# Scaled sums for C2 and decayed B, one bf16 product for the numerators, four-tile K features and loads as list steps in a fused state-space and linear-attention kernel

## The chip, the cores and the metric

One core of a Trainium2 chip. The time is the device time of one execution in microseconds, the median of the runs shown. The kernel is one program without a loop at run time; its engines (TensorE or PE, VectorE or DVE, ScalarE or ACT, GpSimd or POOL, SyncE or SP) each work through their own instructions in order and wait for one another by semaphores.

## What is computed

x has 2048 rows of 512. Two branches work on it, and a gate per row mixes them:

```python
g = sigmoid((x * gate_w).sum(-1))                      # one number per row
# branch A: a diagonal state-space model with complex poles
Lam_bar = exp(dt * Lam);  B_bar = (Lam_bar - 1) / Lam * B
h[t] = Lam_bar * h[t-1] + B_bar @ x[t]
a[t] = 2 * Re(C @ h[t]) + x[t] * Dskip
# branch B: linear attention, 32 heads of 16
pq, pk = q @ w_phi, k @ w_phi                          # per head
phi = concat(softmax(p), softmax(-p))                  # 32 features per head
kv = sum_s phi_k[s] v[s]^T;  z = sum_s phi_k[s]
b = (phi_q @ kv) / (phi_q @ z + 1e-6) @ wo
out = g * a + (1 - g) * b
```

Inputs and output are bf16.

## The kernel before

Rows are split by their index modulo four, so that a tile of 128 rows ("ti", 16 of them) holds rows of one residue, and the recurrence runs as a scan over 512 steps of four rows each. x is loaded transposed (`xT`, DMA transposes on SyncE, L225).

The program is written as small generators, one for each piece of work (`st_k`, `st_g`, `feat_sum`, ...). Each `yield` ends a step. The string `ORDER` (L24) is the list of steps: the loop at L783 takes a token, sets the PSUM banks behind "@" and the engine of a copy or scaling (":D" gives it to VectorE, otherwise ScalarE), and runs the generator to its next yield. So the list fixes the order of every engine's instructions. `F:n` puts n dummy matmuls of 128 columns on TensorE. The pieces that matter here:

- `W`, `f`, `w` fold the 16x16 head matrices into the K and Q weights; `B` (L319) builds the block matrix for that, four products of 128x128.
- `k`, `v`, `q` (L431 to 450) are projections of one tile: four matmuls of 512 columns, then a copy out of PSUM (L117 on ScalarE, L119 on VectorE).
- Features. `x` (L469) is a maximum tree over 16 values in four steps and a subtraction; `n` (L477) the same with minima; `e` (L483) exponentials on ScalarE, one for each tile; `s` (L489) a tree of sums, logarithm and exponential on ScalarE, and the product that normalizes (L500, or L511 for queries, behind which four DMA transposes per group go out on SyncE, L515). K features run for two tiles at a time, eight groups; the first four query tiles also in two groups of two (A, B); the other twelve in three groups of four (X1 to S3). The trees are the lines L464 of the profile.
- `a` (L521) adds a tile's features times values into `kvacc`, and the gate's sums.
- `U`, `P`, `P2`, `P3`, `P4`, `M` compute the poles from the transposed parameters (`vec_n`, `V`); `i` (L400) the rotation tables by sines on ScalarE, with an absolute value on VectorE (L410); `D` (L376) nine sets of diagonal matrices, three products of 1536 elements.
- Decayed B, `LBT`: `p` (L535) multiplies Bn_r and Bn_i by diagonals on TensorE, four matmuls of 256 columns in each of eight steps, and ScalarE copies out (eight copies).
- `g` (L545) applies BrT/BiT and LBT to x into `uv`; `z` (L585) rotates and scans on VectorE; `h` (L617) gets the in-between states.
- C2, the output matrix: `c` (L565), for each of eight parts two matmuls of 512 columns with diagonals and one copy.
- `r`, `b`, `K` derive the matrices for other residues; `y` (L696) forms branch A of a tile in PSUM.
- `o` (L717) is branch B of a tile: numerators and denominators by eight small matmuls in two halves, two logarithms (`ld`), one exponential (`rd`), and on VectorE two products straight from PSUM with the gate's factor RG (L737, 256 elements each), then a DMA transpose on SyncE (L743). `t` (L746) adds the result times Wo to branch A's PSUM, scales by the gate (L754 on ScalarE or L756 on VectorE), and stores.

Loads: before the list runs, ScalarE's queue issues the K weights (`C2r`), `Wc` and `Wv`; SyncE's issues eight x tiles, B twice (plain, and transposed in eight), the other eight x tiles, the Q weights, C and Wo. `vec_n` comes on GpSimd's queue (L256).

Of the kernel before, what the change touches and what calls it, by code (L numbers as in the profile page):

```python
# [10 lines left out]
ALU = mybir.AluOpType  # L11
# [25 lines left out]
a5 z2 g300 xA s6 s7 q2 z2 s6 s7 z2 g301 g300 xA s7 g311 g301 v12 g310@6 xA g311 z1 nA c11@4 z1 nA eA z2 nB s7 z2 c03@7
c12@2 g310 xB g311 eA q15@5 c12 s6 c03 s7 g310 h01@0 nB q15 g310 sA c10@2 z2 s7 h01 c11 c13@7 xB nB v13@5 z3 xB h11@6
z2 c10 z3 a6 z2 sA z2 h11 q9@0 c02@4 v13 sA q9 xB a6 nB c13 h10@2 q6@5 c02 v15@0 z3 q12@7 q10@6 q8@4 xB v15 sA nB
h21@0 q12 z3 h00@7 q6 q10 q5@5 eB q8 s7 q4@6 a7 sA eB q4 z3 z3 h10 z3 c00@4 q7@2 c00 a7 sB sA r1 sB z3 sB z3 h20@6 sA  # L40
K0@4 sB q7 sA sB z3 q13@2 q5 h31@5 h21 q14@0 sB G h20 h30@6 sA sB h00 q13 h31 sA sB sB sB G h30 Y q11@2 END N1 K2@7 X1
Y o0@5 N1 o1@6 r0 K0 o1 Y X1 N1 X1 q11 Y o0 X1 N1 o0@3 X1 N1 o0 o1@4 y1@1 o1 q14 o1 o0 b1 o0 N2 y0@2 o2@0 o0 K2 X2 o0
E1 o1 E1 E1 y1 E1 o2 X2 K3@7 N2 X2 o2@5 o1 y0 o1 y2@3 S1 o2 o2 o2 K1@6 K1 y2 S1 o2 S1 N2 X2 o2 S1 y3@4 o3@0 y0 r1 X2
N2 K3 S1 S1 N2 y3 r0 S1 S1 S1 o3 o3@5 o3 G y1 y3 y7@6 o3 E2 t0 y2 o3 E2 E2 E2 G t1 o3 t0 y5@7 t2 N3 y4@0 t2 y7 b1 X3
r3 o4@5 N3 S1 S2 S2 o4 o4@2 y5 b0 o4 o4 t1 o3 y4 o4 o5@3 o5 o4 b0 S1 o5@5 S2 t3 o5 b3 S1 o5 r2 o5 y4 y6@1 t3 r2 o4 y7
o6@2 t1 b2 S2 r3 o6 o6@3 y6 b2 o7@4 o6 S2 t0 o5 y5 y6 o5 t4 o6 b3 o7 S2 S2 t2 y8@5 o6 X3 o6 S2 y11@2 t4 X3 t4:A o7@0
o7 N3 y10@3 X3 o7 o6 N3 y11 t5 y10 X3 N3 o7 t6 o7 S2 E3 y8 S2 o8@4 E3 E3 o8 o8@0 o8 S2 o8 o7 t5:D t6:D o8 o8 y10 y8
y9@7 o10@1 o9@4 E3 o9 S3 o9@0 S2 o9 o10 o8 o9 o9 y9 S3 t7 S3 o9 t6 o10@4 y11 o9 o10 S3 o10 y9 o10 S3 o10 y14@0 t8 t7
y13@1 S3 S3 t5:A o11@4 y12@6 y13 o11 t8 o10 S3 o11@5 o11 t9 S3 t9:D S3 y14 t3:A o11 t10 o12@7 o11 S3 o11 t10:D o12
o12@4 o12 o12 y14 o12 o13@5 S3 o13 o13@3 y12 o12 o13 t7 t8:A o13 o11 o13 o12 o14@7 o14 o14@4 o13 o14 t9:A y13 o14 y12  # L50
o14 o14 o15@5 o15 o15@3 y15@7 o15 o15 t11 o15 t11 o13 o14 o15 y15 t12 y15 t10 t12 t14 t14 o15 t11 t12 t13 t14:A t15
t15 t13:D t15:A t13
"""
C2_VECTOR = ()
# [14 lines left out]
def kernel(  # L69
# [92 lines left out]
    nc.scalar.dma_start(out=wk_nat[:], in_=B_wqkv[:, D:2 * D].rearrange("(k p) n -> p k n", p=P))  # L162
    nc.scalar.dma_start(out=Wc[:], in_=B_w_phi.rearrange("(k hl) e f -> (hl e) k f", hl=8))
    nc.scalar.dma_start(out=Wv[:], in_=B_wqkv[:, 2 * D:3 * D].rearrange("(k p) n -> p k n", p=P))
# [13 lines left out]
    RG = const.tile([P, NTI], F32, name="RG")  # L178
    ge = const.tile([P, NTI], F32, name="ge")
# [19 lines left out]
    dg = pBC.tile([P, 9, PT, P], BF16, name="dg")  # L199
# [3 lines left out]
    dgv = pBC.tile([P, 9, PT, 4], BF16, name="dgv")  # L203
# [22 lines left out]

    for ti in range(8):
        x_load(ti)
    nc.sync.dma_start(out=Bn_r[:], in_=A_B_re.rearrange("(j p) d -> p j d", p=P))
    nc.sync.dma_start(out=Bn_i[:], in_=A_B_im.rearrange("(j p) d -> p j d", p=P))  # L230
    for kt in range(KT):
        nc.sync.dma_start_transpose(out=BrT[:, kt, :], in_=A_B_re[:, kt * P:(kt + 1) * P])
        nc.sync.dma_start_transpose(out=BiT[:, kt, :], in_=A_B_im[:, kt * P:(kt + 1) * P])
    for ti in range(8, NTI):
        x_load(ti)
    for j in range(KT):
        nc.sync.dma_start_transpose(out=WTq[:, j, :], in_=B_wqkv[:, j * P:(j + 1) * P])
    for kt in range(KT):
        nc.sync.dma_start_transpose(out=CrT[:, kt, :], in_=A_C_re[:, kt * P:(kt + 1) * P])
        nc.sync.dma_start_transpose(out=CiT[:, kt, :], in_=A_C_im[:, kt * P:(kt + 1) * P])  # L240
    nc.sync.dma_start(out=Wo[:], in_=B_wo.rearrange("(k p) n -> p k n", p=P))

# [7 lines left out]
    make_identity(nc, ident[:])  # L250
    nc.gpsimd.iota(iot[:], pattern=[[1, NC]], base=0, channel_multiplier=0, allow_small_or_imprecise_dtypes=True)
    identf = stg.tile([P, P], F32, name="identf", bufs=1)
    make_identity(nc, identf[:])
# [8 lines left out]
    mask16 = stg.tile([P, 8], F32, name="mask16", bufs=1)  # L262
    nc.vector.tensor_reduce(out=mask16[:], in_=identf[:].rearrange("p (g e) -> p g e", e=16), axis=AX.X, op=ALU.add)
# [13 lines left out]
    def st_W(j):  # L277
        pt = bank([P, KT, P], BF16, "ptw")
        for dtile in range(KT):
            nc.tensor.transpose(pt[:, dtile, :], wk_nat[:, dtile, j * P:(j + 1) * P], ident[:])  # L280
        yield
        evac(WTk[:, j, :], pt[:].rearrange("p a b -> p (a b)"))
        yield
# [35 lines left out]
    def st_B():  # L319
        for kt in range(HG):  # L320
            VT(out=BD[:, kt, :].rearrange("p (g f) -> p g f", f=Dh), in0=Wc[:, kt, :].unsqueeze(1).to_broadcast([P, 8, Dh]),
               in1=mask16[:].unsqueeze(2).to_broadcast([P, 8, Dh]), op=ALU.mult)
            yield
# [52 lines left out]
    def st_D():  # L376
        for k0 in (0, 3, 6):
            if k0 == 0:
                nc.vector.tensor_copy(out=dgv[:].rearrange("p k j f -> p (k j) f"),
                                      in_=dgs[:].rearrange("p k j -> p (k j)").unsqueeze(2).to_broadcast([P, 9 * PT, 4]))  # L380
            VT(out=dg[:, k0:k0 + 3].rearrange("p k j (c f) -> p (k j) c f", f=4),
               in0=ident[:].rearrange("p (c f) -> p c f", f=4).unsqueeze(1).to_broadcast([P, 3 * PT, 32, 4]),
               in1=dgv[:, k0:k0 + 3].rearrange("p k j f -> p (k j) f").unsqueeze(2).to_broadcast([P, 3 * PT, 32, 4]), op=ALU.mult)
            yield
# [15 lines left out]
    def st_i(j):  # L400
# [9 lines left out]
        VS(out=kk_[:].bitcast(mybir.dt.uint32), in0=psi[:].bitcast(mybir.dt.uint32), scalar1=0x7FFFFFFF, scalar2=None, op0=ALU.bitwise_and)  # L410
# [4 lines left out]
    pools = {}  # L415

# [41 lines left out]
    def tree(pool, src5, L, op, nm, key, last_dtype=BF16, groups=NB):  # L458
        cur = src5
        n = Dh  # L460
        while n > 1:
            n //= 2
            t = pool.tile([P, L, groups, n, 4], last_dtype if n == 1 else BF16, name=f"{nm}{n}", bufs=(2 if n == 1 else 1))
            VT(out=t[:], in0=cur[:, :, :, 0:n, :], in1=cur[:, :, :, n:2 * n, :], op=op)  # L464
            cur = t
            live[key] = t
            yield

    def feat_max(p, first, L, nm, small, big):  # L469
        X5 = v5(Xq[:, first:first + L, :])  # L470
        yield from tree(small(), X5, L, ALU.max, f"mx{nm}", ("mx", p))
        EE = big().tile([P, L, NB, 2, 64], BF16, name=f"EE{nm}", bufs=3)
        live["EE", p] = EE
        VT(out=half(EE, 0), in0=X5, in1=live["mx", p][:].to_broadcast([P, L, 8, Dh, 4]), op=ALU.subtract)
        yield
# [351 lines left out]
```

## Time and profile before

| what | value |
|---|---|
| runs shown | 167.51, 167.69, 168.19 us; median 167.69 |
| span of the profiled execution (first to last instruction) | 166.1 us |
| median of the runs less this span | 1.6 us |
| VectorE instructions, busy | 354, 143.7 us |
| ScalarE instructions, busy | 236, 114.8 us |
| TensorE matmuls, busy | 1088, 157.6 us |
| granted TensorE clock, mean | 0.994 |

In the views of the profile a row of a timeline is start, length, engine, line, operation, tiles, shape and count, with idle time and its releaser in brackets. SPq and ACTq are the DMA-issuing instructions of SyncE and ScalarE. A group's row gives the busy time and the mean of one instruction in ns. Times of the profile are those of one execution.

### The profile page before, as it was taken

To read this page: it belongs to the slowest core of one execution; us is meant where nothing else is said; L and a number is where in the kernel's file an instruction comes from. 1 tells how busy PE (TensorE), PEld (TensorE's weight loads), DVE (VectorE), ACT (ScalarE), POOL (GpSimd) and SP (SyncE) were. 2 spreads that over 40 slices of the span, in tenths; PEclk is the share of its full clock that TensorE was granted. 3 is DMA by queue.
4 is the path that set the end of the run, shared out by engine and by line. 5 is a ranking of instruction groups with operands and counts; after the bars stand their busy time and mean duration, and the time that the engine had idled before them with its cause. 6 is when DMAs were issued, how large, how long until landed. Compare 5 with 4: busy or idle time off the path is not lost.

```text
span 166.1 us, 3051 instructions
## 1 busy us (share of the span) xinstructions
PE 157.6 (95%) x1088; PEld 82.3 (50%) x1109; DVE 143.7 (87%) x354; ACT 114.8 (69%) x236; POOL 9.6 (6%) x28
## 2 busy tenths in 40 slices
PE   7689999999999999999999999999999999999990
PEld 7444455455465454454454554545446445445440
DVE  4379999999999999999999999999999996818410
ACT  3389999999898268578965966876888356423331
POOL 8218200000000000000000000000000000000000
PEclk9999999999999999999999999999999999999997
DMA  4969945464444200000000019212296585478542
GB/s 111 267 121 281 142 99 97 95 98 95 95 105 85 98 0 6 0 0 0 0 4 0 0 24 181 52 32 63 65 132 154 162 189 129 119 174 216 128 125 95
DMA packets 50830, 15.94 MB, mean 96 GB/s; under 512 B 46208, under 2 KB 50816, under 8 KB 50816
## 3 DMA queue, kind: packets, MB, share of 16 engines
q1 hardware_dynamic: 48064, 13.77, 39.8%
q10 hardware_dynamic: 2592, 1.98, 4.4%
q8 instruction: 8, 0.13, 0.3%
q14 instruction: 6, 0.05, 0.1%
q0 software_dynamic: 160, 0.01, 0.1%
HBM read 2.64 MB, written 2.10 MB: 29 GB/s over the span
## 4 chain that ended last, share of the span: by engine, by line
PE 84%; DVE 8%; DMA 3%; POOL 2%; issue 1%; ACT 1%; POOLq 0%
PE pgq L552 8%; PE py L750 8%; PE pgq L555 8%; PE py L705 8%; PE pq L429 8%; PE py L706 8%; PE pv L429 5%; PE py L712 4%; PE pk L429 4%; DMA vec_n<-in_A_log_dt_dram 3%; PE kvacc L527 3%; PE pn L728 3%; PE pk L674 2%; PE pk L675 2%; DVE psi L406 2%; DVE mxk L464 1%
## 5 line engine op out<-in xcount | busy, mean ns | idle before, releaser
L429 PEld LDWEIGHTS <-xT 128*128 128x128 bf16 x192 | 18.1, 97 | 20.8 <-DMA xT<-in_A_x_dram 0.7
L136 ACT ACTIVATE EEk<-EEk 128x1024 bf16<-128x1024 bf16 x20 | 21.0, 1070 | 0.8 <-DVE EEk L480 0.8
L737 DVE SCALAR_TENSOR_TENSOR on<-pn,RG,rd 128x256 bf16<-128x256 f32 x32 | 14.4, 474 | 3.2 <-ACT rd L136 1.7
L429 PE MATMUL pv<-Wv,xT 128*128 128x512 bf16 x62 | 16.0, 379 | 0.3 <-DMA xT<-in_A_x_dram 0.2
L750 PE MATMUL py<-Wo,oT 128*128 128x512 bf16 x62 | 15.8, 379 | 0.1
L555 PE MATMUL pgq<-xT,LBT 128*128 128x512 bf16 x60 | 15.5, 379 | 0.2
L429 PE MATMUL pq<-Wq,xT 128*128 128x512 bf16 x61 | 15.6, 379 | 0.1
L429 PE MATMUL pk<-Wk,xT 128*128 128x512 bf16 x61 | 15.1, 379 | 0.2
L136 ACT ACTIVATE EEq<-EEq 128x1024 bf16<-128x1024 bf16 x12 | 11.8, 1044 | 3.3 <-DVE EEq L480 3.3
L136 ACT ACTIVATE ld<-pn 128x16 f32<-128x16 f32 x32 | 4.7, 182 | 12.6 <-PE pn L728 12.6
L706 PE MATMUL py<-Wv,H 128*128 128x512 bf16 x31 | 11.7, 379 | 0.1
L705 PE MATMUL py<-Wk,H 128*128 128x512 bf16 x31 | 11.7, 379 | 0.1
L705 PE MATMUL py<-C2r,H 128*128 128x512 bf16 x31 | 11.7, 379 | 0.0
L117 ACT CAST Xq<-pq 128x512 bf16<-128x512 f32 x16 | 9.2, 589 | 3.6 <-PE pq L429 3.4
L117 ACT CAST uv<-pgq 128x512 bf16<-128x512 f32 x16 | 9.3, 588 | 3.4 <-PE pgq L560 2.3
L706 PE MATMUL py<-C2i,H 128*128 128x512 bf16 x30 | 11.4, 379 | 0.1
L756 DVE TENSOR_SCALAR ot<-py,G 128x512 bf16<-128x512 f32 x5 | 3.7, 747 | 8.4 <-PE py L750 8.4
L117 ACT CAST vx<-pv 128x512 bf16<-128x512 f32 x15 | 8.7, 598 | 2.6 <-PE pv L429 2.6
L754 ACT ACTIVATE ot<-py,G 128x512 bf16<-128x512 f32 x11 | 7.4, 678 | 4.5 <-PE py L750 4.5
L117 ACT CAST Xq<-pk 128x512 bf16<-128x512 f32 x16 | 9.2, 601 | 1.4 <-PE pk L429 1.4
L464 DVE TENSOR_TENSOR smk<-smk 128x512 bf16<-128x512 bf16 (+2 forms) x30 | 9.8, 327 | 0.0
L500 DVE TENSOR_TENSOR EEk<-EEk,rck 128x2048 bf16<-128x2048 bf16 x8 | 9.7, 1214 | 0.0
(179 smaller groups left out, 348.6 us busy)
## 6 DMA issues: line engine op xcount, KB each, us to landing
out_dram<-ot SPq DMA_DIRECT2D x9, 128.0 KB, 2.1
out_dram<-ot ACTq DMA_DIRECT2D x7, 128.0 KB, 2.1
C2r<-in_B_wqkv_dram ACTq DMA_DIRECT2D x1, 512.0 KB, 4.4
Wv<-in_B_wqkv_dram ACTq DMA_DIRECT2D x1, 512.0 KB, 5.9
Bn_r<-in_A_B_re_dram SPq DMA_DIRECT2D x1, 512.0 KB, 5.1
Bn_i<-in_A_B_im_dram SPq DMA_DIRECT2D x1, 512.0 KB, 6.0
Wo<-in_B_wo_dram SPq DMA_DIRECT2D x1, 512.0 KB, 3.8
xT<-in_A_x_dram SPq DMA_TRANSPOSE x16, 3.9
```

The source lines that it names most:

```text
L117: nc.scalar.copy(out=out_ap, in_=in_ap)
L136: ins = nc.scalar.activation(**kw)
L429: MM(out=pt[:], lhsT=xT[:, kt, ti * P:(ti + 1) * P], rhs=W[:, kt, :], start=(kt == 0), stop=(kt == KT - 1))
L464: VT(out=t[:], in0=cur[:, :, :, 0:n, :], in1=cur[:, :, :, n:2 * n, :], op=op)
L500: VT(out=E5, in0=E5, in1=rc[:].to_broadcast([P, L, 2 * NB, Dh, 4]), op=ALU.mult)
L552: MM(out=pgq[:], lhsT=BT[:, kt, js], rhs=xT[:, kt, r1 * NC:(r1 + 1) * NC], start=(kt == 0), stop=False)
L555: MM(out=pgq[:], lhsT=LBT_[:, kt, js], rhs=xT[:, kt, (r1 - 1) * NC:r1 * NC], start=False, stop=(r1 == 1 and kt == KT - 1))
L705: MM(out=py[:], lhsT=src[:, j, 0, off:off + P], rhs=cr[:, j, :], start=(j == 0), stop=False)
L706: MM(out=py[:], lhsT=src[:, j, 1, off:off + P], rhs=ci[:, j, :], start=False, stop=False)
L737: nc.vector.scalar_tensor_tensor(out=on[:, 2 * hf:2 * hf + 2].rearrange("p g h e -> p (g h) e"), in0=pns[hf][:, :, 0:Dh], scalar=RG[:, ti: ...
L750: MM(out=py[:], lhsT=oT[:, g, :], rhs=Wo[:, g, :], start=False, stop=(g == HG - 1))
L754: nc.scalar.mul(out=ot[:], in_=py[:], mul=G[:, ti:ti + 1])
```

## The change

What is computed stays as above; these parts are done otherwise:

1. **C2 and decayed B** no longer go through TensorE. `scaled_sum` makes two bf16 copies scaled by a factor per partition (ScalarE, or VectorE with ":D") and VectorE adds them. Decayed B is made in its natural layout in K0T's space and brought to `LBT` by a DMA transpose on SyncE, eight in all. Of the 32 scaled copies seven carry ":D". Only three of nine sets of diagonals are still made.
2. **Numerators** are copied out of PSUM to bf16 (`nu`), by ScalarE or, for 10 of the 32 halves, all in o8 and o10 to o15, by VectorE; the gate's factor goes into the exponential's bias; one bf16 product of 512 elements replaces the two.
3. **K features** run in groups of two, two, four, four and four tiles, the first query group in one of four. A tree keeps its steps in one tile.
4. **Loads** of B, C, Q weights, Wo, Wv and of the x tiles 8 to 15 become steps of the list. K weights come in two halves, Wc is first on SyncE, plain B and Wv on ScalarE's queue.
5. The block matrix is one product; three of four absolute values stay on VectorE, one goes to ScalarE.
6. The list is new: 832 tokens for 866, K tiles ahead of V tiles, 52 dummy matmuls for 45.

```diff
-        for hf in range(2):
-            nc.vector.scalar_tensor_tensor(out=on[:, 2 * hf:2 * hf + 2].rearrange("p g h e -> p (g h) e"),
-                                           in0=pns[hf][:, :, 0:Dh], scalar=RG[:, ti:ti + 1],
-                                           in1=rd[:, hf].unsqueeze(2).to_broadcast([P, 16, Dh]), op0=ALU.mult, op1=ALU.mult)
-            yield
+            evac(nu[:, hf], pn[:, :, 0:Dh])
+            yield
+        aexp(out=rd[:], in_=ld[:], func=ACT.Exp, scale=-1.0, bias=nge[:, ti:ti + 1])
+        yield
+        VT(out=on[:].rearrange("p g h e -> p (g h) e"), in0=nu[:].rearrange("p a h e -> p (a h) e"),
+           in1=rd[:].rearrange("p a h -> p (a h)").unsqueeze(2).to_broadcast([P, 32, Dh]), op=ALU.mult)
+        yield
...
+    KG = ((0, 2), (2, 2), (4, 4), (8, 4), (12, 4))
...
+    def scaled_sum(k, out_ap, a, b, ca, cb):
+        ta, tb = mtmp[k % NTMP]
+        for t_, x_, c_ in ((ta, a, ca), (tb, b, cb)):
+            if sel["eng"] == "act":
+                nc.scalar.mul(out=t_, in_=x_, mul=c_)
+            else:
+                VS(out=t_, in0=x_, scalar1=c_, scalar2=None, op0=ALU.mult)
+            yield
+        VT(out=out_ap, in0=ta, in1=tb, op=ALU.add)
+        yield
+
+    def st_p(j):
+        for ri, (ka, kb) in enumerate(((DG_LR, DG_NLI), (DG_LI, DG_LR))):
+            lbn = K0T[:, (2 * j + ri) % 4, :]
+            yield from scaled_sum(2 * j + ri, lbn, Bn_r[:, j, :], Bn_i[:, j, :], dgs[:, ka, j:j + 1], dgs[:, kb, j:j + 1])
+            nc.sync.dma_start_transpose(out=LBT[:, :, ri, j * P:(j + 1) * P], in_=lbn)
+            yield
...
     def st_c(dst, j):
-        pc = bank([P, D], F32, "pc")
-        MM(out=pc[:], lhsT=dg[:, da, j, :], rhs=CrT[:, j, :], start=True, stop=False)
-        MM(out=pc[:], lhsT=dg[:, db, j, :], rhs=CiT[:, j, :], start=False, stop=True)
-        yield
-        evac(d_[:, j, :], pc[:])
-        yield
+        yield from scaled_sum(2 * j + dst, d_[:, j, :], CrT[:, j, :], CiT[:, j, :], dgs[:, da, j:j + 1], dgs[:, db, j:j + 1])
...
     def feat_max(p, first, L, nm, small, big):
-        EE = big().tile([P, L, NB, 2, 64], BF16, name=f"EE{nm}", bufs=3)
+        EE = big().tile([P, 4, NB, 2, 64], BF16, name=f"EE{nm}", bufs=EEB[nm])[:, 0:L]
...
     def st_B():
+        VT(out=BD[:].rearrange("p k (g f) -> p k g f", f=Dh), in0=Wc[:].unsqueeze(2).to_broadcast([P, HG, 8, Dh]),
+           in1=mask16[:].unsqueeze(1).unsqueeze(3).to_broadcast([P, HG, 8, Dh]), op=ALU.mult)
```

Two rows of the list before and two of the new one, where K features are formed, and the rows with the first loads and the last features of the new one:

```
k11 a1 s2 g010@4 n4 k10 a1 s2 g011@7 n4 x4 s2 n4 x4 n4 s3 g010 g011 s2 x4 s3 x4 n4 x5 k12@2 s3 p02 s2 e4 n5 k13@6 x5
e4 s3 x5 s2 n5 s3 g010 g011 s4 a2 k12 g011 x5 n5 s3 p32@5 k13 s4 n5 a2 s3 x5 n5 x6 g010 z0 s4 w0@2 n6 w0 p32 v9@7 w3@6
...
B R0 R3 R2 F:40 l8 W0@0 W1@1 W1:D W2@2 W2:D l9 W3@3 W3:D f1@4 W0 f0@5 f0:D LV f2@6 f1 f3@0 f3:D f2 k0@1 k0 NR V@2 V U
...
I2 n2 s1 k13@4 k13 g010@5 g010 e2 e2 e2 p1 e2 a1 a1 x3 x3 I0 k12@0 x3 x3 x3 v10 k14@7 I1 k15@1 g011@4 k14 g001@3
g101@7 n3 p0 k15 n3 n3 k12 n3 n3 g001 s2 s2 s2 s2 v11@1 x4 x4 x4 n4 n4 n4 p1 p2 e3 Q1 e3 g001 s2 s2 s2 g011 p3 g011 e3
...
t4:A o10:D o10@0 o8 o10 o9 S3 t7 o10 y9@0 y9 t7 y13@4 S3 S3 o10 y9 o10 o11@2 S3 S3 S3 t8 S3 o11 o11@2 o11:D o11 o11 t9
y12@2 y12 t8 t8:A t1:A t9:D t9:A o12@5 o12 o12@0 y11 o12:D o12 o12 o11 t2:A t6:A o13@5 o13:D t7:A o13@0 o13:D o13 t10
```

A token R, I, C, Q, l, LV, NR, NI or O is one load (B transposed, C, Q weights, x tile, Wv, plain B, Wo); the fourth token of `p` and the seventh of `o` are DMA transposes.

More of the change, by code (lines that the diff above doesn't have):

```diff
@@ L198 @@
     phT0 = pBC.tile([P, 4, NB, P], BF16, name="phT0")
-    dg = pBC.tile([P, 9, PT, P], BF16, name="dg")
+    dg = pBC.tile([P, 3, PT, P], BF16, name="dg")
+    NTMP = 4
+    mtmp = [phT0[:, k].rearrange("p (a m) f -> p a (m f)", a=2) for k in range(NTMP)]
+    mtmp = [(m_[:, 0, :], m_[:, 1, :]) for m_ in mtmp]
     DG_NLI, DG_LR, DG_LI, DG_NMI, DG_MR, DG_MI, DG_NBR, DG_NBI, DG_BR = range(9)
@@ L202 @@
     dgs = pBC.tile([P, 9, PT], F32, name="dgs")
[L203 removed]
+    dgv = pBC.tile([P, 3, PT, 4], BF16, name="dgv")
     Bn_r = pBC.tile([P, PT, D], BF16, name="Bn_r")
@@ L225, in x_load @@
         nc.sync.dma_start_transpose(out=xT[:, :, ti * P:(ti + 1) * P], in_=x_res[ti // 4, ti % 4])
+    make_identity(nc, ident[:])
+    identf = stg.tile([P, P], F32, name="identf", bufs=1)
+    make_identity(nc, identf[:])
+    mask16 = stg.tile([P, 8], BF16, name="mask16", bufs=1)
+    nc.vector.tensor_reduce(out=mask16[:], in_=identf[:].rearrange("p (g e) -> p g e", e=16), axis=AX.X, op=ALU.max)
     for ti in range(8):
         x_load(ti)
[L229 to L241, printed above, removed]
     fk_g = tc.tile_pool(name="featK", bufs=3, reuse_waits="tile")
@@ L456, in v5, with tree @@
         return ap3.rearrange("p l (hh f hl) -> p l hh f hl", hh=8, f=Dh)
-    def tree(pool, src5, L, op, nm, key, last_dtype=BF16, groups=NB):
+    def tree(pool, src5, L, op, nm, key, last=None, groups=NB):
+        t = pool.tile([P, 4, groups, Dh // 2, 4], BF16, name=f"{nm}8", bufs=1)[:, 0:L]
         cur = src5
@@ L462, in tree @@
             n //= 2
-            t = pool.tile([P, L, groups, n, 4], last_dtype if n == 1 else BF16, name=f"{nm}{n}", bufs=(2 if n == 1 else 1))
-            VT(out=t[:], in0=cur[:, :, :, 0:n, :], in1=cur[:, :, :, n:2 * n, :], op=op)
+            dst = last if n == 1 and last is not None else t[:, :, :, 0:n, :]
+            VT(out=dst, in0=cur[:, :, :, 0:n, :], in1=cur[:, :, :, n:2 * n, :], op=op)
             cur = t
-            live[key] = t
+            live[key] = dst
             yield
@@ L490, in feat_sum @@
         EE = live["EE", p]
-        E5 = EE[:].rearrange("p l hh s (f hl) -> p l (hh s) f hl", f=Dh)
-        yield from tree(small(), E5, L, ALU.add, f"sm{nm}", ("sm", p), last_dtype=F32, groups=2 * NB)
-        lg = small().tile([P, L, 2 * NB, 1, 4], F32, name=f"lg{nm}", bufs=(2 if L == 2 else 1))
-        aexp(out=lg[:], in_=live["sm", p][:], func=ACT.Ln)
+        E5 = EE.rearrange("p l hh s (f hl) -> p l (hh s) f hl", f=Dh)
+        sm = small().tile([P, 4, 2 * NB, 1, 4], F32, name=f"sm{nm}1", bufs=2)[:, 0:L]
+        yield from tree(small(), E5, L, ALU.add, f"sm{nm}", ("sm", p), last=sm, groups=2 * NB)
+        lg = small().tile([P, 4, 2 * NB, 1, 4], F32, name=f"lg{nm}", bufs=1)[:, 0:L]
+        aexp(out=lg, in_=sm, func=ACT.Ln)
         yield
         if ph is None:
-            rc = small().tile([P, L, 2 * NB, 1, 4], BF16, name=f"rc{nm}", bufs=2)
-            aexp(out=rc[:], in_=lg[:], func=ACT.Exp, scale=-1.0)
+            rc = small().tile([P, 4, 2 * NB, 1, 4], BF16, name=f"rc{nm}", bufs=2)[:, 0:L]
+            aexp(out=rc, in_=lg, func=ACT.Exp, scale=-1.0)
             yield
-            VT(out=E5, in0=E5, in1=rc[:].to_broadcast([P, L, 2 * NB, Dh, 4]), op=ALU.mult)
+            VT(out=E5, in0=E5, in1=rc.to_broadcast([P, L, 2 * NB, Dh, 4]), op=ALU.mult)
             yield
             return
-        lg5 = lg[:].rearrange("p l (hh s) o hl -> p s (l hh) (o hl)", s=2)
+        lg5 = lg.rearrange("p l (hh s) o hl -> p s (l hh) (o hl)", s=2)
         dl = small().tile([P, L * NB, 4], F32, name=f"dl{nm}")
@@ L519, in acc @@
         return live["acc"][m // 4][:, m % 4 * KVW:(m % 4 + 1) * KVW]
+    KG = ((0, 2), (2, 2), (4, 4), (8, 4), (12, 4))
     def st_a(n):
-        for u in range(2):
-            ti = 2 * n + u
-            if ti == 0:
+        for u in range(KG[n][1]):
+            nt = KG[n][0] + u
+            ti = nt
+            if nt == 0:
                 live["acc"] = [bank([P, 512], F32, f"kvacc{b}") for b in range(2)]
@@ L624, in st_h @@
             MM(out=ph[:], lhsT=ident[:], rhs=U1[:, ri, :], start=True, stop=False)
-        MM(out=ph[:], lhsT=dg[:, da, j, :], rhs=H3[:, j, 0, prev], start=add, stop=False)
-        MM(out=ph[:], lhsT=dg[:, db, j, :], rhs=H3[:, j, 1, prev], start=False, stop=True)
+        MM(out=ph[:], lhsT=dg[:, da - 3, j, :], rhs=H3[:, j, 0, prev], start=add, stop=False)
+        MM(out=ph[:], lhsT=dg[:, db - 3, j, :], rhs=H3[:, j, 1, prev], start=False, stop=True)
         yield
@@ L634, in st_G @@
     def st_G():
-        VS(out=ge[:], in0=live["acc"][1][:, 4 * KVW:4 * KVW + NTI], scalar1=-Z_MAX, scalar2=None, op0=ALU.max)
+        VS(out=nge[:], in0=live["acc"][1][:, 4 * KVW:4 * KVW + NTI], scalar1=-Z_MAX, scalar2=-1.0, op0=ALU.max, op1=ALU.mult)
         yield
-        aexp(out=RG[:], in_=ge[:], func=ACT.Exp, scale=-1.0)
+        aexp(out=G[:], in_=nge[:], func=ACT.Exp)
         yield
-        VS(out=G[:], in0=RG[:], scalar1=1.0, scalar2=None, op0=ALU.add)
+        VS(out=G[:], in0=G[:], scalar1=1.0, scalar2=None, op0=ALU.add)
         yield
```

172 lines of the change are left out of this document (78 added, 94 removed).

## The prediction

> **What bounds the kernel now.** I read the page first: busy time of each engine, the chain that ended last, and then the stretches of ten microseconds.
>
> ```profile
> PE 157.6 (95%) x1088; PEld 82.3 (50%) x1109; DVE 143.7 (87%) x354; ACT 114.8 (69%) x236; POOL 9.6 (6%) x28
> PE 84%; DVE 8%; DMA 3%; POOL 2%; issue 1%; ACT 1%; POOLq 0%
> ```
>
> TensorE looks like the bound. The windows say that it is not alone (columns: stretch, length, busy PE, PEld, DVE, ACT):
>
> ```profile
> 30.00:40.00 10.00, 9.95 (x86) 5.33 (x86) 10.00 (x31) 9.94 (x18) 0.00 (x0) 1.00 0.51 96
> 90.00:100.00 10.00, 9.95 (x69) 4.92 (x68) 10.00 (x21) 8.10 (x16) 0.00 (x0) 1.00 0.09 17
> 130.00:140.00 10.00, 9.95 (x68) 4.93 (x68) 8.61 (x17) 5.42 (x12) 0.00 (x0) 1.00 0.72 171
> 150.00:160.00 10.00, 9.95 (x73) 5.09 (x73) 4.75 (x11) 3.54 (x14) 0.00 (x0) 1.00 0.64 165
> ```
>
> From 11 to 130 us VectorE has no idle time either; only the last 35 us are TensorE's alone. So a change that takes matmuls away is worth what VectorE lets through, and I work out VectorE's stage: from its first table operation (L402, 11.35 us) to the last product of the last query group (L511, below), and then the tail behind it.
>
> How close VectorE's operations stand is read from its timeline (start, length):
>
> ```profile
> 14.43 0.46 DVE L464 TENSOR_TENSOR mxk<-Xq 128x512 bf16<-128x512 bf16 x1
> 14.93 0.29 DVE L464 TENSOR_TENSOR mxk<-mxk 128x256 bf16<-128x256 bf16 x1
> ...
> 29.48 0.42 DVE L464 TENSOR_TENSOR smk<-smk 128x512 bf16<-128x512 bf16 x1
> 29.82 0.42 DVE L464 TENSOR_TENSOR mxk<-Xq 128x512 bf16<-128x512 bf16 x1
> ```
>
> The second reads what the first wrote and starts 0.035 us after its end (14.89). The fourth belongs to another tree and starts 0.08 us before the third ends. It is so throughout: an operation that reads its direct neighbour's output starts 0.034 us after its end, the rest about 0.08 us before it. Dependent neighbours cost 0.114 us a pair. The list of before has 8 of them up to the L511 product; it interleaves its trees.
>
> **The sum up to that product.** I go down both lists and add each VectorE operation's row less 0.08 us, or plus 0.034 for a dependent neighbour. Before: 325 operations, 134.5 us. VectorE is late by 7.95 us at the first table operation (11.35, with 3.4 of the work done) and idles 2.2 us between 130 and 145. That gives 144.65; the trace has the end at 145.3, so 0.6 is left over. The change:
>
> - K features and the first query group as quads: eight of the ten two-tile groups become four of four tiles. The maximum tree with its subtraction takes 1.40 us for two tiles (419, 283, 214, 200, 683 ns, less 5 x 80) and 2.41 for four (Q rows: 683, 413, 282, 214, 1215), so a quad saves 0.39; the minimum the same; the sum 0.35 (product of 4096 by extension from 1214 at 2048: 2.28). 4 x 1.13 = **-4.5**.
> - Diagonals, two of three products of 952 ns go: -1.75. Four block products of 283 become one of 512 elements at the same rate: -0.2. One of four absolute values moves to ScalarE: -0.34. Together **-2.3**.
> - Copies out of PSUM that the list now gives VectorE: one W and two f more, one v less: **+0.95**.
> - C2 and decayed B: 16 additions of 128x512 bf16 (417, L597): 16 x 0.337 = 5.4. Seven of 32 scaled copies carry ":D". No row shows a bf16 scaled copy; it lies between 182 (128x64) and 416 (L410, 512 of 32 bits). I take 290, in the middle, 7 x 0.21 = 1.5, and keep 0.8 either way. **+6.9**.
> - Numerators: 22 products of 474 become 11 of 512 elements and two copies of 256 from PSUM (418, L648). The new product reads a bf16 value sixteen times over. Ends: 417 (dense bf16) and 678 (L629, one element a cycle). I take 678, because the block product L321 repeats an operand in the same pattern and runs at that rate (128 in 283), though its mask is f32. 22 x 0.394 = 8.7 against 7.3: **-1.4**; with 417, another -2.9.
> - One more scaled output on VectorE: **+0.67**.
> - Dependent neighbours: the new list runs its trees in one piece ("s2 s2 s2 s2 x4 x4 x4 n4 n4 n4"). I count 79 pairs, 71 more than before: 71 x 0.114 = **+8.1**.
>
> Sum **+8.4**: 142.9 us.
>
> The Trainium skill ("VectorE: DVE Perf Modes", The DRAIN you can't avoid) says that eight copies with a semaphore after each took as long as with one at the end, so that chaining costs nothing and only the number of operations counts. By that rule the last item is 0 and the time that of rival A below. The trace above disagrees, 0.035 after against 0.08 before.
>
> The start: the parameters' transposes wait for vec_n, which lands at 8.8 us as before (3.47 + 5.29, on the chain). Behind it the parameter operations stand in one piece at 0.2 us each, so the first table operation comes at 11.7; but 5.5 us of work is done by then, since four evacuations lie ahead of it. Lag 6.2 instead of 7.95. Of the 2.2 us of waits I keep 1, since VectorE is now behind the others, and the 0.6 left over. **End of the last L511 product: 6.2 + 142.9 + 1.6 = 150.7**, against 145.3.
>
> **The tail behind it.** The product in VectorE's timeline, then SyncE's queue and ScalarE's end:
>
> ```profile
> 144.07 1.22 DVE L511 TENSOR_TENSOR EEq<-EEq,rhoq 128x2048 bf16<-128x2048 bf16 x1 [0.38 <-ACT rhoq L136]
> ...
> 145.35 5.33 SPq L515 DMA_TRANSPOSE phT<-EEq  x4
> 150.78 0.53 SPq L758 DMA_DIRECT2D out_dram<-ot  x1
> 151.40 5.25 SPq L743 DMA_TRANSPOSE oT<-on  x4
> ...
> 162.20 0.69 ACT L754 ACTIVATE ot<-py,G 128x512 bf16<-128x512 f32 x1 [1.04 <-PE py L750]
> ```
>
> Four feature transposes and the five of o11 to o15 follow one another at 1.31 us; both lists have these nine. The ninth is issued 10.5 us behind the product, lands 2.3 later (12.8); four matmuls 0.86, the output copy 0.69, and 3.2 from there to the end of the span (162.89 to 166.1): 17.6. Before it was 20.8, because TensorE still had its backlog; now TensorE has 6.5 us less. **Span 150.7 + 17.6 = 168.3. The median of the runs lies 1.6 above the span (167.69 against 166.1): 169.9 us.**
>
> **What is off this path.** TensorE loses 32 matmuls of 256 columns (0.108 start to start) and 16 of 512 (0.216): -6.9, and gains 7 fillers of 0.056. Alone it would end 6.5 earlier, span 159.6; I cost this at nothing because VectorE's 8.4 lies across it. The eight new transposes of decayed B on SyncE wait for additions; when VectorE's first sum is due (about 20.6) SyncE is still at work on Wc, eight x tiles and eight more loads of 1.3 us, up to some 22.4; TensorE, ahead of VectorE by some 5 us, covers that. x, C and B loads as list steps come behind those waits; the last ones are used at about 80 us, and the queue's own work before them is 59 us. K first needs one x tile per 0.86 us of matmuls where tiles come each 1.33; what that idles is TensorE's, with the same cover. If the cover is gone, each comes on top.
>
> **Rivals.**
> (A) Faster. The dependent neighbours cost nothing here, because the pairs' gaps fall where VectorE would wait anyway. Place: VectorE from 20 to 150 us. Price: 8.1 us, so 150.7 becomes 142.6, span 160.2, just above TensorE's 159.6: **161.8**. It decides once more than 2.2 of the 8.1, some 19 pairs, vanish. For it: 87% against 95% busy on the page. Against it: no idle time there before, and 0.114 in every pair that I found. The Trainium skill's rule above ("VectorE: DVE Perf Modes", The DRAIN you can't avoid) would lead here.
> (B) The new product runs two elements a cycle: -2.9, **167.0**, no change. The Trainium skill ("Vector Engine (DVE) Microarchitecture Reference", 5.1 Performance modes) says that one 2-byte element read 16 times by a two-source operation ran at one a cycle; no run here shows it yet.
> (C) ScalarE becomes late. It takes 25 scaled copies (about 0.64 each by L660's 715) for 16 evacuations (0.53): +7.5 us; from 15 to 42 us it was full (9.94 above). If half falls there, VectorE waits 3.7: **173.6**.
>
> **How the numbers follow.** Forecast 0.55, A 0.18, B 0.15, C 0.12. Half a per cent is about what a measurement of this kernel can tell from no change: 166.9 to 168.5. A and a third of B are faster: 0.23. The rest of B and the low edge of the forecast are the same: 0.15. Slower 0.62. The forecast's own range is 167.8 to 172, from the copies' price (0.8), the waits (0 to 3) and the kept remainder. The range for 8 in 10 goes from A's 161.8 to C's 173.6: 161.8 to 174.
>
> **What would show it.** Right: VectorE without idle time to about 150 us and TensorE with several microseconds of it between 60 and 110; gaps of 0.034 in the trees; `on` at about 680 ns; the last L511 product (its new line) about 151. Wrong: that product before 146 (A), `on` near 420 (B), VectorE waiting for ScalarE in the first 60 us (C), or x or transposed B landing late with TensorE then setting the end.

## The result, and the profile after

| | before | predicted | after |
|---|---|---|---|
| time, median of the runs (us) | 167.94 (167.51 to 168.25) | 169.9 | 187.69 (186.48 to 188.37) |
| span of the profiled execution | 166.1 | 168.3 | 186.6 |
| first table operation on VectorE | 11.35 | 11.7 | 20.14 |
| end of the last product of the last query group | 145.3 | 150.7 | 163.2 |
| from there to the end of the span | 20.8 | 17.6 | 23.4 |

The ratio is 1.118 (95% interval 1.112 to 1.124). The change is slower, as forecast, but by 20 us instead of 2, far outside the range. The span is 18.3 us longer than predicted: 8.4 of them are there before the first table operation, 4.1 come between it and the last product, 5.8 behind it. The first table operation, before and after:

```profile
11.35 0.49 DVE L402 TENSOR_SCALAR kk<-iot,ssm_par 128x512 f32<-128x512 f32 x1
...
20.14 0.49 DVE L413 TENSOR_SCALAR kk<-iot,ssm_par 128x512 f32<-128x512 f32 x1
```

The page of after, busy times and then the chain that ended last:

```profile
PE 158.2 (85%) x1049; PEld 78.9 (42%) x1068; DVE 151.8 (81%) x306; ACT 126.8 (68%) x258; POOL 9.9 (5%) x28
DMA 7%; PE 3%; SPq 1%; ACT 0%; issue 0%
```

VectorE has 48 instructions fewer and is busy 8 us longer; no engine is near full. The same stretches as before, and 10 to 20 us (columns: stretch, length, busy PE, PEld, DVE, ACT, POOL, granted clock, DMA share, GB/s):

```profile
10.00:20.00 10.00, 4.08 (x10) 1.33 (x11) 2.23 (x14) 1.76 (x4) 0.00 (x0) 0.66 0.76 148
...
30.00:40.00 10.00, 8.63 (x44) 3.94 (x43) 9.55 (x28) 9.97 (x16) 0.00 (x0) 1.00 0.29 62
...
90.00:100.00 10.00, 9.62 (x85) 5.10 (x86) 9.90 (x23) 9.46 (x17) 0.00 (x0) 1.00 0.01 2
...
130.00:140.00 10.00, 9.30 (x58) 4.64 (x57) 9.90 (x18) 6.94 (x14) 0.00 (x0) 1.00 0.28 60
...
150.00:160.00 10.00, 9.28 (x63) 4.36 (x62) 8.14 (x12) 6.22 (x16) 0.00 (x0) 1.00 0.73 144
```

From 30 to 150 us it looks as predicted: VectorE full but for small gaps, TensorE with idle time. What was not predicted is the first row: from 8.8 to 14.6 us VectorE, TensorE and ScalarE all stand. ScalarE's timeline there:

```profile
6.02 0.58 ACT L115 COPY Xq<-ptw 128x512 bf16<-128x512 bf16 x1 [2.84 <-PE ptw L266]
14.63 0.39 ACTq L296 DMA_DIRECT2D Wv<-in_B_wqkv_dram  x1
15.06 1.07 ACT L115 CAST Wk<-pf 128x512 bf16<-128x512 f32 x2 [8.46 <-DMA BrT<-in_A_B_re_dram]
```

The longest waits of after say who waits for whom (total, times, longest):

```profile
DVE vec L303 <- PE pvt L301: 8.5, 1, 8.5
ACT Wk L115 <- DMA BrT<-in_A_B_re_dram: 8.5, 1, 8.5
...
PE pk L444 <- ACT Wk L115: 7.0, 1, 7.0
```

Read from below: the K projections wait for two Wk copies; these stand on ScalarE behind the issue of Wv (token LV); that issue waits until the first transpose of B has landed. Wv has nothing to do with B. In the compiled program every DMA of the two queues signals one of eight semaphores, and an issue waits until the transfer that used its semaphore before has landed; Wv got that of BrT. BrT stands on SyncE behind eight x tiles and is issued at 11.81; it lands 2.80 us later, at 14.61, and the issue of Wv follows at 14.63. Bn_i, another of the three loads, has the semaphore of the third transpose of B and is issued at 21.19, when that has landed. The transpose of the parameters comes behind the K projections on TensorE, so VectorE waits too. The Trainium skill ("DMA: Bandwidth & Descriptors", Anatomy of one DMA) says that DMA engines don't wait on semaphores, the issuing sequencer does, before dispatch; the row at 14.63 agrees, 8.0 us after the copy ahead of it.

The neighbours on VectorE, as the prediction had them: the second reads what the first wrote and starts 0.03 after its end (90.72), the third is independent and starts 0.08 before the second ends (91.18):

```profile
90.03 0.69 DVE L622 TENSOR_TENSOR ms<-w,T2s 128x1024 bf16<-128x1024 bf16 x1
90.75 0.43 DVE L624 TENSOR_TENSOR H<-mc,ms 128x512 bf16<-128x512 bf16 x1
91.10 0.42 DVE L563 TENSOR_TENSOR C2r<-phT 128x512 bf16<-128x512 bf16 x1
```

The tail: the last product (L528 is the L511 of before), SyncE's queue, and the last output:

```profile
161.97 1.22 DVE L528 TENSOR_TENSOR EEq<-EEq,rhoq 128x2048 bf16<-128x2048 bf16 x1
```

```profile
158.86 6.46 SPq L753 DMA_TRANSPOSE oT<-on  x3
165.43 4.89 SPq L532 DMA_TRANSPOSE phT<-EEq  x3
170.41 1.24 SPq L753 DMA_TRANSPOSE oT<-on  x1
171.74 1.32 SPq L532 DMA_TRANSPOSE phT<-EEq  x1
173.16 6.50 SPq L753 DMA_TRANSPOSE oT<-on  x4
```

```profile
182.79 0.69 ACT L764 ACTIVATE ot<-py,G 128x512 bf16<-128x512 f32 x1 [1.01 <-PE py L760]
```

The first feature transpose comes 2.2 us behind the product instead of at once, the nine end at 179.66, 16.5 behind it, where nine at 1.31 would take 11.8.

### The profile page after: what moved, and what is told of

Its sections match the earlier page's. It is cut to its first block, busy times and chain, and to the rows that moved or that the text cites. A ratio compares the mean times of both kernels' runs of the same rounds, so it can differ in the third digit from the quotient of the medians.

```text
span 186.6 us, 2958 instructions
## 1 busy us (share of the span) xinstructions
PE 158.2 (85%) x1049; PEld 78.9 (42%) x1068; DVE 151.8 (81%) x306; ACT 126.8 (68%) x258; POOL 9.9 (5%) x28
## 5 line engine op out<-in xcount | busy, mean ns | idle before, releaser
L444 PE MATMUL pk<-Wk,xT 128*128 128x512 bf16 x62 | 17.3, 410 | 9.0 <-ACT Wk L115 7.0
L134 ACT ACTIVATE EEk<-EEk 128x1024 bf16<-128x1024 bf16 x20 | 20.1, 1055 | 0.5 <-DVE EEk L496 0.5
L583 PE MATMUL pgq<-xT,LBT 128*128 128x512 bf16 x62 | 16.2, 379 | 0.1
L134 ACT ACTIVATE ld<-pn 128x16 f32<-128x16 f32 x32 | 5.9, 189 | 12.2 <-PE pn L740 11.5
L748 DVE TENSOR_TENSOR on<-nu,rd 128x512 bf16<-128x512 bf16 x16 | 10.9, 684 | 0.5
L740 PE MATMUL pn<-KVm,phT 128*128 128x68 bf16 x128 | 7.4, 195 | 4.1 <-DMA phT<-EEq 3.3
L740 PEld LDWEIGHTS <-phT 128*128 128x128 bf16 x128 | 6.1, 97 | 10.5 <-DMA phT<-EEq 6.6
L117 DVE CAST nu<-pn 128x256 bf16<-128x256 f32 x10 | 4.1, 422 | 7.9 <-ACT ld L134 7.9
L717 PEld LDWEIGHTS <-H 128*128 128x128 bf16 x64 | 6.2, 98 | 8.3 <-issue 2.1
L616 DVE TENSOR_TENSOR_SCAN w<-ssm_par,ut 128x512 bf16<-128x512 f32 x8 | 9.5, 1214 | 0.0
```

Source lines behind the costliest of these rows:

```text
L117: nc.vector.tensor_copy(out=out_ap, in_=in_ap)
L134: ins = nc.scalar.activation(**kw)
L444: MM(out=pt[:], lhsT=xT[:, kt, ti * P:(ti + 1) * P], rhs=W[:, kt, :], start=(kt == 0), stop=(kt == KT - 1))
L583: MM(out=pgq[:], lhsT=LBT_[:, kt, js], rhs=xT[:, kt, (r1 - 1) * NC:r1 * NC], start=False, stop=(r1 == 1 and kt == KT - 1))
L616: nc.vector.tensor_tensor_scan(out=w[:, ri, :], data0=rb, data1=ut[:, ri, :], initial=0.0, op0=ALU.mult, op1=ALU.add)
L717: MM(out=py[:], lhsT=src[:, j, 0, off:off + P], rhs=cr[:, j, :], start=(j == 0), stop=False)
```

## The experiments

All are compared with the kernel before on the same chip. "Interleaved run" is the fifth below.

**Loads: Wv first.** Wv is issued at the top of ScalarE's queue.

```diff
+    nc.scalar.dma_start(out=Wv[:], in_=B_wqkv[:, 2 * D:3 * D].rearrange("(k p) n -> p k n", p=P))
     nc.sync.dma_start(out=Wc[:], in_=B_w_phi...)
...
     def st_LV():
-        nc.scalar.dma_start(out=Wv[:], ...)
         yield
```

> The kernel after, with the load of Wv issued at the top of ScalarE's queue, behind the two halves of C2r, as before. Theory 1 (the start hole is ScalarE standing at the issue of Wv until 14.63 us, with the two Wk copies behind it): the first table operation (L413) comes at about 11.7 us instead of 20.14, and the time falls by the 8.4 us of the hole, from 187.7 to 179.3. Theory 2 (the hole comes from the x tiles, Wc or B loads on SyncE's queue, or from K going first): the first table operation stays near 20, the time at 186 to 188. In between, if another late load takes over part of the hole: 181 to 185.

Measured 185.16 (ratio 1.102, 1.098 to 1.107). Only 2.5 us came back, because the next load took the place:

```profile
15.85 0.38 ACTq L277 DMA_DIRECT2D Bn_r<-in_A_B_re_dram  x1
16.28 0.20 ACT L134 ACTIVATE ssm_par<-vec 128x4 f32<-128x4 f32 x1 [6.82 <-DMA BrT<-in_A_B_re_dram]
```

Now the first parameter exponential stands behind the issue of Bn_r, which waits for a B transpose as well.

**Loads: Wv on SyncE.** The token LV stays where it is, with `nc.sync` for `nc.scalar`.

> The kernel after, with the load of Wv at the same place of the list, but on SyncE's queue, behind x tile 9. Nothing is loaded earlier; only the engine that stands at the issue differs. Theory 1 (what costs is that ScalarE stands): first table operation about 11.7 us, Wv lands near 22 us so that the V projections come late, time 179 to 181. Theory 2 (what costs is that a load lands late): no gain, 186 to 188.

Measured 190.42 (1.133, 1.129 to 1.137), slower than after. Neither theory had that. ScalarE stood at Bn_r as in the run before (until 17.18), and Wv was issued only at 19.35, so that TensorE stood for it:

```profile
25.74 1.89 PE L444 MATMUL pv<-Wv,xT 128*128 128x512 bf16 x4 [13.19 <-DMA Wv<-in_B_wqkv_dram]
```

So theory 1 in its narrow form (only the engine that stands matters) falls: the late landing costs too. The group of four took 1.89 us here against 1.03 elsewhere; the granted clock from 20 to 30 us was 0.50, in the idle time and behind it.

**Loads: the late Wv alone, in the kernel before.** Wv is issued behind the two copies of `W` on ScalarE, with the first transpose of B ahead of it. (SyncE's later loads are written behind Wv in the program, so that Wv gets the semaphore of that transpose; their order on SyncE is as before.)

```diff
-... W3@3 B W3 B F:8 ...
+... W3@3 B W3 LV B F:8 ...
```

> The kernel before, in which the load of Wv alone is moved: on ScalarE's queue behind the evacuations of the transposed weights, where its issue waits for the first transpose of B, due at about 15 us; everything else as before. Theory 1: ScalarE's parameter exponentials and weight copies wait there, the first table operation moves from 11.35 to about 17 us, and the time goes from 167.9 to 173 to 176. Theory 2 (the hole belongs to the new loads or to K first): within 1 us of 167.9.

Measured 183.36 (1.089, 1.083 to 1.094): +15.4, twice what was expected. The issue came at 18.05, the first table operation at 21.04, and then VectorE stood once more, since the list of before has V projections first, which wait for Wv:

```profile
30.31 0.42 DVE L469 TENSOR_TENSOR mxk<-Xq 128x512 bf16<-128x512 bf16 x1 [6.18 <-ACT Xq L117]
```

One moved load, with nothing else of the change, is enough for a loss of this kind.

**No load left on ScalarE's list.** Wv first as above, and both plain loads of B on SyncE right behind the first eight x tiles, as before.

```diff
     for ti in range(8):
         x_load(ti)
+    nc.sync.dma_start(out=Bn_r[:], ...)
+    nc.sync.dma_start(out=Bn_i[:], ...)
...
     def st_N(ri):
-        nc.scalar.dma_start(out=(Bn_r, Bn_i)[ri][:], ...)
         yield
```

> The kernel after with no load left in ScalarE's list: Wv at the top of its queue (as in the run with Wv first) and both loads of B (Bn_r, Bn_i) on SyncE's queue right behind the first eight x tiles, as before. Theory 1 (ScalarE stands at issues that wait for the B transposes; with Wv gone Bn_r took the place, at 15.85 us): first table operation about 11.7 us, the whole 8.4 us comes back: 178 to 180. Theory 3 (behind the first stall stands a second limit, x tiles and V projections that come late between 10 and 40 us): 181 to 185, first table operation at 11.7 all the same.

Measured 178.62 (1.061, 1.058 to 1.064), 9.1 less than after:

```profile
12.14 0.49 DVE L414 TENSOR_SCALAR kk<-iot,ssm_par 128x512 f32<-128x512 f32 x1
...
153.96 1.22 DVE L529 TENSOR_TENSOR EEq<-EEq,rhoq 128x2048 bf16<-128x2048 bf16 x1
```

The first table operation is at 12.14 and the last product 8.0 earlier. Theory 1 holds, with all three loads in it.

**The interleaved run.** The run above with its list's tree steps moved by at most 14 places: the same instructions, 30 instead of 79 dependent neighbours. Part of one row of the list:

```diff
-a1 a1 x3 x3 I0 k12@0 x3 x3 x3 v10 k14@7 ... g101@7 n3 p0 k15 n3 n3 k12 n3 n3 g001 s2 s2 s2 s2 v11@1 x4 x4 x4
+a1 a1 x3 n3 x3 I0 k12@0 n3 x3 n3 x3 n3 x3 v10 k14@7 ... g101@7 p0 k15 k12 n3 g001 s2 x4 s2 x4 s2 x4 s2 v11@1
```

> The run with the loads off ScalarE, and its list with the trees interleaved: steps of other trees are moved by at most 14 places, so that 30 instead of 79 dependent neighbours are left on VectorE; the same instructions on every engine. If a dependent neighbour costs 0.114 us (gap +0.034 instead of -0.08) and VectorE sets the time: 49 x 0.114 = 5.6 us less than that run, so about 173.5. If neighbours cost nothing: within 1 us of it.

Measured 173.06 (1.030, 1.025 to 1.035), 5.6 less, as expected. The last product:

```profile
147.96 1.23 DVE L529 TENSOR_TENSOR EEq<-EEq,rhoq 128x2048 bf16<-128x2048 bf16 x1
```

Between the first table operation and this product the trace has 71 gaps of 0.02 to 0.06 us in after and in the run with the loads moved, 23 here, 7 in before. 5.56 / 48 = 0.116 us each; the prediction had 0.114 from two rows. The Trainium skill's sentence that a semaphore after each of eight copies cost nothing extra ("VectorE: DVE Perf Modes", The DRAIN you can't avoid) does not carry over to this list.

**Scaled copies all on ScalarE.** In the interleaved run the seven ":D" copies of decayed B lose their ":D".

> The interleaved run with the seven scaled copies of decayed B that VectorE did (0.35 us each) given to ScalarE (0.64 each). VectorE loses 7 x 0.27 = 1.9 us, ScalarE gains 4 between 20 and 40 us, where it is at 9.89 of 10. If VectorE sets the stage and ScalarE has room: 171.2. If ScalarE is late there, as rival C had it: 173 to 177.

Measured 176.14 (1.051, 1.047 to 1.054), 3.1 us more by the medians. VectorE lost 2.4 us of work and waited for ScalarE instead:

```profile
DVE smk L481 <- ACT EEk L134: 1.9, 1, 1.9
...
DVE K0T L564 <- ACT phT L560: 1.4, 1, 1.4
```

This is rival C's mechanism. With seven copies on VectorE, as the change has them, it did not decide.

**Numerators alone, in the kernel before.** Copies on ScalarE, one product, as in the diff of the change.

> The kernel before with one part of the change alone: the numerators copied out of PSUM by ScalarE and one bf16 product of 128x512 (0.684 us in the trace of after) instead of two products of 0.474 us from PSUM; 13 instead of 14 output tiles, two numerator tiles. By VectorE's ledger up to the last product of the last query group, 22 x 0.394 = 8.7 becomes 11 x 0.604 = 6.6: -2.1 us. If VectorE alone sets the time: 165.8. If TensorE closes it anyway (busy 95% of the span): 167 to 168.2. If ScalarE's 32 copies of 0.37 us lie on the chain of the tail: up to 170.

Measured 169.72 (1.010, 1.006 to 1.014), 1.8 more. The ledger's 2.1 us are there (in the stage VectorE's durations fall by 2.9, less 0.08 of overlap for each of 11 operations fewer: 2.0), but VectorE waits for the longer work on ScalarE:

```profile
DVE on L735 <- ACT rd L135: 4.3, 6, 1.3
```

In before such waits are 1.7 us, two of them.

**C2 alone, in the kernel before.**

```diff
-        MM(out=pc[:], lhsT=dg[:, da, j, :], rhs=CrT[:, j, :], start=True, stop=False)
-        MM(out=pc[:], lhsT=dg[:, db, j, :], rhs=CiT[:, j, :], start=False, stop=True)
+        for t_, x_, c_ in ((ta, CrT[:, j, :], dgs[:, da, j:j + 1]), (tb, CiT[:, j, :], dgs[:, db, j:j + 1])):
+            nc.scalar.mul(out=t_, in_=x_, mul=c_)
         yield
-        evac(d_[:, j, :], pc[:])
+        VT(out=d_[:, j, :], in0=ta, in1=tb, op=ALU.add)
```

> The kernel before with one part of the change alone: C2 by two scaled copies on ScalarE and one addition of 128x512 bf16 on VectorE (0.417 us) instead of two matmuls and an evacuation; the nine diagonals stay. TensorE loses 16 matmuls at 0.216 = 3.5 us, VectorE gains 8 x 0.337 = 2.7, ScalarE some 6. If TensorE alone sets the time of before: 167.9 - 3.5 = 164.4. If VectorE does up to the last product: 170.6. If both share it (TensorE's backlog lies in the tail): 167 to 170.

Measured 174.58 (1.038, 1.032 to 1.042): worse than all three forecasts. The copies come in runs on ScalarE, between 80 and 90 us:

```profile
80.00:90.00 10.00, 6.04 (x31) 2.45 (x30) 9.11 (x21) 9.72 (x18) 0.00 (x0) 0.83 0.00 0
```

ScalarE is full, TensorE, which was to gain 3.5 us, stands for 4 in this stretch alone, and VectorE waits for the copies (0.9 twice). Four copies of 0.7 in a row hold up everything that ScalarE evacuates behind them. Up to the last product VectorE's work grows by 2.8 us, as priced, and its waits over 0.06 us by 2.9.

**The tail, six runs on the interleaved one.** Ten oT buffers instead of eight; the fourth of the last feature transposes right behind the third; the same with five stores moved behind the last transpose; these stores moved alone; two of the four transposes on ScalarE's queue; and half the data in these four. Two of the edits:

```diff
-        oT = op_.tile([P, HG, P], BF16, name="oT", bufs=8)
+        oT = op_.tile([P, HG, P], BF16, name="oT", bufs=10)
```

> The interleaved run, with ten instead of eight buffers for the transposed outputs oT. In the tail of after one oT transpose stood 1.84 us at SyncE for TensorE's read of the buffer's earlier content, with the last feature transposes behind it. If that wait sets the tail: 1.5 to 2.2 us less than the interleaved run. If the wait is covered, or only moves to the next waiting transpose: the same within 0.5.

172.87 (1.029): the same. In the interleaved run itself the first feature transpose already followed its product at once (149.25), so this wait was no longer there to be taken.

> The interleaved run, in which the last of the four feature transposes of the last query group stands right behind the third, instead of behind the transpose of o11. Behind the last product SyncE's queue is then four feature transposes and five output transposes, as the prediction counted them. In the interleaved run the last feature transpose is issued 7.5 us behind the product and the tail is 22.4 us. If its place sets the end: 1.3 us less, about 171.8. If each issue waits for o12 to o15's own numerators anyway: the same within 0.5 as 173.1.

174.42 (1.040, 1.037 to 1.043): 1.4 more by the medians. Four feature transposes and then five output transposes, as the prediction counted them, is not the better order: TensorE's list has the product of o11's output ahead of o15's numerators, and o11's transpose, now behind all four, lands only at 161.65:

```profile
157.35 4.30 DMA oT<-on
```

> The run before it in this list, with five stores of finished outputs (t1, t2, t6, t7, t9) on ScalarE's queue moved behind the last output transpose; in the interleaved run such stores were under way while three feature transposes took 6.05 us instead of 4.0. If the stores slow the transposes or ScalarE stands at their issue: 2 us less, about 170. If they don't: the same within 0.5, or up to 1 more, since the stores now end last.

172.62 (1.033, 1.027 to 1.039), 1.8 less by the medians than the run before it (one of the four runs took 174.37), about what was expected of stores that slow transposes. The same stores moved in the interleaved run itself:

> The interleaved run with the five stores t1, t2, t6, t7, t9 behind the last output transpose, and the feature transposes where the interleaved run has them. With the fourth feature transpose moved forward, taking these stores away from the transposes was worth 1.8 us by the medians, and the four feature transposes took 6.26 instead of 7.76 us of SyncE's queue. If stores and transposes slow one another in the tail: about 171.3 here too, 1.8 under the interleaved run's 173.1. If that gain only undid the worse order: the same as 173.1 within 0.5.

172.74 (1.030, 1.027 to 1.033) against the interleaved run's 1.030: the same. But the tail is not the same inside. SyncE's queue at the end, of the interleaved run and then of this one:

```profile
158.14 6.46 SPq L754 DMA_TRANSPOSE oT<-on  x4
164.70 2.86 SPq L769 DMA_DIRECT2D out_dram<-ot  x4
```

```profile
157.52 5.30 SPq L754 DMA_TRANSPOSE oT<-on  x4
162.91 5.33 SPq L769 DMA_DIRECT2D out_dram<-ot  x4
```

Without those stores beside them the transposes are through 1.8 us earlier (162.82 against 164.60), and the last stores take the gain back. In these runs moving transfers about in the tail changes who waits, not the end.

> The interleaved run with two of the four last feature transposes (the second and the fourth) issued on ScalarE's queue instead of SyncE's. In the tail of after the chain goes through two feature transposes of 4.6 and 4.5 us from issue to landing, with the DMA engines at 0.86 of their time. If SyncE's issue (1.31 us each, one behind the other) sets the tail: 2 to 3 us less than the interleaved run's 173.1, about 170.5. If the transfers themselves do: the same within 0.7. If ScalarE standing at the two issues delays the numerators' copies: 1 to 2 us more.

181.4 (1.078, 1.071 to 1.084): 8 more. This is the third case, far beyond its 1 to 2 us, and it leaves open which of the first two holds. The compiled program makes a transpose on one queue wait for the earlier ones of the other, and ScalarE has to stand at these issues (5.9 and 3.2 us idle around them), with the logarithms and numerator copies of the outputs behind them.

```diff
-                nc.sync.dma_start_transpose(out=dst(u), in_=EE[:, u]...)
+                nc.sync.dma_start_transpose(out=dst(u)[:, 0:4, :], in_=EE[:, u, 0:4]...)
```

> The interleaved run, in which the four feature transposes of the last query group carry half their data (four of eight head groups; the other half of the buffer is set to a constant, so that o12 to o15 are computed from half the features). The number of issues on SyncE's queue and every wait stay. In the tail of the interleaved run feature transposes took 4.4 us from issue to landing in the median, in that of before 2.8. If the transfers themselves, with the DMA engines full, set the tail: 2 to 4 us less than the interleaved run's 173.1, so 169 to 171. If the issues, the waits for numerators or the chain of engines set it: within 1 us of 173.1.

171.22 (1.022, 1.018 to 1.027): 1.8 us less by the medians. The DMA issues between 140 us and the end (size, median us from issue to landing), of the interleaved run and then of this one:

```profile
oT<-on SPq DMA_TRANSPOSE x9, 3.2
phT<-EEq SPq DMA_TRANSPOSE x6, 4.4
```

```profile
oT<-on SPq DMA_TRANSPOSE x9, 2.5
phT<-EEq SPq DMA_TRANSPOSE x6, 3.2
```

In before the two have 2.4 and 2.8. With half the data in four transposes all of them land sooner, those of the outputs too, and here nothing takes it back. So the transfers that fall together in the tail are worth some 2 us of it.

## Why the prediction was wrong, point by point

- **VectorE sets the end up to the last product.** Right, once the start is mended: taking 48 dependent pairs off VectorE alone, with all instructions kept, gave 5.6 us.
- **The ledger.** Nearly right in sum. Between the first table operation and the last product the operations with their overlaps take 139.5 us in after and 132.2 in before, +7.3 by the gaps of the traces; the prediction's two lists give 137.4 and 131.1, +6.3. `on` took 684 ns (678 taken), so rival B is out; an addition 417 to 425; the scaled copy 350, above the 290 taken, 0.4 us in all. Waits over 0.06 us were 3.6 instead of the 1.6 kept. The 2.0 of the waits and the 2.1 by which 139.5 exceeds 137.4 make the 4.1 of the stage.
- **Dependent neighbours, +8.1.** Right in mechanism and size (0.116). Rival A is out.
- **The start: "the first table operation comes at 11.7".** This is the step that failed, with "loads as list steps" costed at nothing. I followed each queue for when a load lands and who uses it, and looked at SyncE, where issuing hurts nobody but transfers. I did not ask, for the three loads put on ScalarE, what their issue waits for, and what stands behind it on an engine that computes. It measured 8.4 us in the trace and 9.1 in the run without it. The "cover" of 5 us that TensorE was to give does not help: TensorE itself waited for ScalarE.
- **The tail, 17.6.** Failed by 5.8 us. I let the pace of SyncE's issues set it: nine transposes at 1.31 us, so that the ninth is issued 10.5 behind the product. In after it is issued 15.3 behind it, because it waits for o15's own product on VectorE, and the numerators of o15 wait until the fourth feature transpose has landed. That landing, 4.5 us, is not in the sum at all:

```profile
171.74 4.53 DMA phT<-EEq
...
178.47 3.20 DMA oT<-on
```

  The steps of the tail, read from the traces (us):

  | | after | interleaved | half the data |
  |---|---|---|---|
  | last product to the first feature transpose | 2.2 | 0.1 | 0.1 |
  | to the issue of the fourth | 6.3 | 7.5 | 6.3 |
  | to its landing | 4.5 | 4.5 | 2.7 |
  | to the issue of the ninth transpose | 2.2 | 2.2 | 2.7 |
  | to its landing (2.3 taken) | 3.2 | 3.2 | 3.2 |
  | to the end of the span | 5.0 | 4.9 | 4.9 |
  | tail | 23.4 | 22.3 | 19.9 |

  In after the first one stands behind an output transpose, and another output transpose lies between the third and the fourth. From the first issue to the fourth, four issues at 1.31 would be 5.2; why they take 6.3 and 7.5 is open. With half the data the queue and the landing are 2.9 us shorter than in the interleaved run and the tail 2.5. That the end hangs on these steps is read from the traces; only the run with half the data tests it. Other buffers, orders and places of the stores didn't shorten the time.
- **TensorE −6.5, off the path.** It did get idle time, as forecast. That this cannot be cashed in is seen where C2 is changed alone: fewer matmuls, 6.3 us slower.
- **Rival C (ScalarE late).** Not the forecast's failure, but nearer than its chance of 0.12 said: of the two parts tried alone in the kernel before, each cost time, and part of it through waits for ScalarE. The sign that the prediction gave for it, VectorE waiting for ScalarE in the first 60 us, did come in after, but there ScalarE stood at an issue (busy 1.76 us from 10 to 20) and was not full.
- **Where the change stands without its two faults.** With the loads off ScalarE and the trees interleaved it is 173.1, still 3% above before: its last product ends 3.9 us later (149.2 against 145.3), and the tail is 1.5 longer. No version tried beat the kernel before.

## What to carry to other kernels

A load that is moved onto the queue of an engine that computes has to be priced by its issue, not by its landing: find what the issue waits for, a reused DMA semaphore too, and what stands behind it on that engine; keep such issues at the top, or on a queue that only moves data, early enough to land in time (late on SyncE's queue the same load gave 190.42 us). In a list for one in-order engine, put an independent operation between producer and consumer: 0.116 us a pair is 5.6 us over 48. And price transposes at the end of a kernel by when they land, with as many in flight as there will be, and by what the last of them waits for, not by the pace of their issue.

## What was not expected of the hardware

- An issue of a load stood on ScalarE for 8 us for a transfer that has no data in common with it (14.63 in after; 15.85 for the next load when the first was moved).
- The granted clock fell to 0.50 in TensorE's holes and came back only some 4 us behind them: matmuls began again at 15.70 in after, at 25.74 with Wv on SyncE and at 23.74 with the late Wv in the kernel before, and the clock was at 0.53, 0.50 and 0.50 in the stretches from 18 to 20, 28 to 30 and 26 to 28 us and at 1.00, 0.98 and 0.97 in the next two us each.
- A feature transpose of 128x1024 bf16 landed 2.8 us after its issue in the tail of before and 4.4 in that of the interleaved run, where more transfers fell together.
